# Sparse attention and feed-forward kernel: a pair's value loads requested one step later

## The chip, the cores and the metric

The kernel runs on one core of a Trainium2 chip. A core has a matrix engine (TensorE, PE; its weight loads are listed apart as PEld), a vector engine (VectorE, DVE), a scalar engine (ScalarE, ACT), a general one (GpSimd, POOL) and one that issues transfers (SyncE, SP). Sixteen DMA engines move data between the memories. The metric is the device time of one execution in microseconds; the time given is the median of three runs.

## What is computed

Attention for 4 batches and 8 heads over 768 positions, head size 64, where a query block of 32 positions looks at its neighbours, at the first and last block, and at three sampled blocks; the first and last query block look at everything. The result goes through a feed-forward layer of 512, 2048 and 512 columns. Queries, keys and values are float32; the two weight matrices come as 64-bit floats.

```python
scores = scale * np.matmul(q, k.transpose(0, 1, 3, 2))
scores = np.where(mask, scores, -1000000000.0)
attn = softmax(scores)                 # written out in the reference
x = np.matmul(attn, v)                 # heads put side by side: 3072 x 512
h = x @ w_in
g = h * (1.0 / (1.0 + np.exp(-1.702 * h)))
out = g @ w_out
```

## The kernel before

**Units, items, entries.** Two neighbouring query blocks are a unit of 64 positions. A unit of one batch is an item. Items go in twos: the items of two batches at the same positions use one entry of keys (`kent`) and one of values (`vent`), which below is called a pair. Eight units, 512 rows, are a chunk; there are six chunks. The first chunk is the first four pairs (entries 0 to 3), the fifth pair (entry 4) is items 8 and 9 and begins the second chunk.

**A pair's values** are three transfers: `gather` makes two indirect ones on POOL (L256), 128 rows of 4 KB each, 512 KB, by sampled row numbers into `vown`; `load_own` makes a plain one on SP (L251), 64 rows of 4 KB, 256 KB, into `vmid`. The rows of the first and last block in `vmid` stay between loads. **A pair's keys** (`load_k`) are nine requests on SP: the queries `qt` (L209), two of `kg` (L213, L214), six single sampled blocks (L227), each with a number read from memory first. Entries from the fifth on share two buffers; a pair may be requested when the pair that had its buffer before has been used.

**Order.** The order of all instructions is written out, engine by engine. `first` runs the attention of the first chunk by a table; it also requests the fifth pair's keys. Then `run` goes through steps: `tick(m)` computes one sixteenth of a chunk's feed-forward layer (one block of 128 of the 2048 columns: `up` at L572 to L574, `gate`, and for the step before it `down`, at L617 in the first eight steps), and between these the attention of the next chunk, item by item as `plan` has set it: scores (L304), transposes (L355), products with the values (L379), a turn (L444). Item 8's values are in step 3, item 9's in step 5.

**Loads.** In every quarter of a step `begin` calls `loads`, which requests all pairs that are free, keys and values in turn, up to the entry number in `self.most`. At first it is five for both, so that in step 0 only the fifth pair's values are requested. Before step 1 (`m == 1`) the limit is lifted.

**Weights.** `weights` is a generator that fetches the blocks of both weight matrices by POOL (L477, 512 KB each, into `win` or one of three buffers `raw`) and turns their 64-bit numbers into a high and a low 32-bit part by ACT (L489, L534) and DVE (L493 to L521). `tick` pulls it a few places at a time, between the other work; a place that begins a block also issues the request five blocks ahead. A converted second-matrix block is stored to `ws` by SP (L527).

**Queues.** An engine takes its instructions in order, a request that waits for a buffer included. The profile lists POOL's requests under the DMA queue q0 and SP's under q1.

Of the kernel before, what the change touches and what calls it, by code (L numbers as in the profile page):

```python
# [43 lines left out]
FIRST = CU // 2  # L44
# [5 lines left out]
class Kernel:  # L50
# [4 lines left out]
    def __init__(self, ctx, tc, q, qd, kb, kT, v, vd, sb, w_in, w_out, out):  # L55
        self.tc, self.nc = tc, tc.nc
        self.q, self.qd, self.kb, self.kT, self.v, self.vd, self.sb = q, qd, kb, kT, v, vd, sb
        self.w64, self.out = (w_in.bitcast(I32), w_out.bitcast(I32)), out
        pool = lambda name, bufs, **k: ctx.enter_context(tc.tile_pool(name=name, bufs=bufs, **k))
        self.const = pool("const", 1)  # L60
        self.work = pool("work", 2)
        self.small = pool("small", 6)
        psum = pool("psum", 1, space=PSUM)
        dram = pool("dram", 1, space=DRAM)
        self.ws = [dram.tile([P, DM], F32, name=f"ws{f}") for f in range(NF)]
        self.bank = [psum.tile([P, 512], F32, name=f"bank{i}") for i in range(8)]
        c = self.const


        self.sbr = c.tile([1, NB, NR, 2], I32, name="sbr")  # L70
        self.zero = c.tile([P, 1], F32, name="zero")
        self.seen = c.tile([P, 2 * NPAIR], F32, name="seen")
        self.ident = c.tile([P, P], F32, name="ident")
        self.vidx = c.tile([P, 2, NB], I32, name="vidx")
        self.bias = c.tile([P, NU, 8], F32, name="bias")
        c.tile([P, 56], F32, name="pad")

        self.kg = [c.tile([P, 12, 2, NPAIR * BLK], F32, name=f"kg{i}") for i in range(RING)]
        self.qt = [c.tile([P, 2, NPAIR * UT], F32, name=f"qt{i}") for i in range(RING)]
        self.vown = [c.tile([P, 2, 2 * DM], F32, name=f"vown{i}") for i in range(RING)]  # L80
        self.vmid = [c.tile([P, 2 * DM], F32, name=f"vmid{i}") for i in range(RING)]
        self.win = [None] * NF
        self.x = [tuple(c.tile([P, NCT, CT], F32R, name=f"x{part}0") for part in ("hi", "lo"))]


        more = c.tile([P, 2 * NCT * CT], F32, name="x1")
        nk, nq = 24 * NPAIR * BLK, 2 * NPAIR * UT
        for flat in (more[:, 0:nk], c.tile([P, 2 * WRING * DM], F32, name="wout")):
            self.kg.append(flat.rearrange("p (n b c) -> p n b c", n=12, b=2))
        self.qt += [more[:, nk + nq * i:nk + nq * (i + 1)].rearrange("p (b c) -> p b c", b=2) for i in range(2)]  # L90
        c.tile([P, 16], F32, name="shift")
        spare = [c.tile([P, 2 * DM], F32, name=f"win{NF - 1 - i}") for i in range(6)]
        self.vblocks = [[t[:, j] for j in range(2)] for t in self.vown] + [spare[0:2], spare[2:4]]
        self.vmid += spare[4:6]
        self.kmidof, self.vmidof = [None] * FIRST, [None] * FIRST
        self.units, self.kent, self.vent, self.items = [], [], [], []

        def entry(of, **more):
            of.append({"n": len(of), "scores": 0, "values": 0, **more})
            return of[-1]  # L100

        def item(k, v, **more):
            k["scores"] += 1
            v["values"] += 1
            self.items.append({"n": len(self.items), "unit": self.units[-1], "k": k, "v": v, **more})

        for b0 in range(0, B, 2):
            for u in range(NU):
                k, v = (entry(of, b=b0, u=u) for of in (self.kent, self.vent))
                for b in (b0, b0 + 1):  # L110
                    entry(self.units, b=b, u=u)
                    item(k, v, first=True, end=True)
            for b in (b0, b0 + 1):
                entry(self.units, b=b, u=None)
                k = entry(self.kent, b=b, u=None)
                for i in range(2):
                    v = entry(self.vent, b=b, u=None, i=i)
                    for half in range(2):
                        item(k, v, i=i, half=half, first=i + half == 0, end=i + half == 2)
        for of in (self.kent, self.vent):  # L120
            for e in of:
                e["at"] = e["n"] if e["n"] < FIRST else e["n"] % RING
        self.knext = self.vnext = FIRST
        self.most = {"scores": FIRST + 1, "values": FIRST + 1}
        self.early, self.turned = True, False


# [782 lines left out]
```

## Time and profile before

| what | value |
|---|---|
| median of 3 runs | 759.45 us (758.43 to 759.71) |
| the profiled execution | 758.66 us, span 757.0 us |
| PE busy | 729.5 us, 96% of the span |
| DVE busy | 406.4 us, 54% |
| ACT busy | 374.9 us, 50% |
| POOL busy | 68.5 us, 9% |
| DMA | 126.87 MB, mean 168 GB/s |
| granted PE clock | 0.996 |

The span is the time from the first to the last instruction of the profiled execution. Times below are counted from its start. PE is the engine that is busy longest; a share of busy time is a mean over the first chunk, the steps and the end, so the rows below are of single stretches.

### The profile page before, as it was taken

The page shows a single profiled execution, that of the slowest core. Times are in us where ns is not written, and L with a number is a line of the kernel's source. Part 1 is how long each engine was busy: PE and PEld are TensorE (multiplying, and loading weights), DVE is VectorE, ACT ScalarE, POOL GpSimd, SP SyncE. Part 2 cuts the span into 40 slices and gives each one's busy share as a digit, 9 for nine tenths or more (in the row PEclk, how much of TensorE's full clock was granted, in tenths as well). Part 3 has the DMA queues.
Part 4 walks back from the last instruction along what each step waited for, and adds up shares of the span by engine and source line. Part 5 has one row for each costly group of instructions (what it writes and reads, how often), then busy time and mean ns, then how long its engine had stood idle before and what let it go on. Part 6 is the DMA issues. An engine that isn't in the chain of part 4 may idle for free.

```text
span 757.0 us, 18902 instructions
## 1 busy us (share of the span) xinstructions
PE 729.5 (96%) x7424; PEld 562.2 (74%) x7424; DVE 406.4 (54%) x1069; ACT 374.9 (50%) x938; POOL 68.5 (9%) x111
## 2 busy tenths in 40 slices
PE   3879999999999999999999999999999999999997
PEld 1555666777787777778878878878777777888885
DVE  4578988885554434554454554454555444443333
ACT  3666666764554443545445445445545444433232
POOL 5422212020000000000000000000000000000000
PEclk9999999999999999999999999999999999999999
DMA  8998996676742547565445465345564331141111
GB/s 263 318 389 294 347 310 211 229 227 180 256 162 71 162 140 228 148 174 169 127 126 168 133 173 169 124 125 170 165 216 157 92 101 32 39 112 43 53 45 55
DMA packets 64250, 126.87 MB, mean 168 GB/s; under 512 B 7617, under 2 KB 30402, under 8 KB 63650
## 3 DMA queue, kind: packets, MB, share of 16 engines
q1 hardware_dynamic: 51922, 83.72, 36.5%
q0 software_dynamic: 11376, 41.03, 16.0%
q8 instruction: 58, 0.95, 0.5%
q10 hardware_dynamic: 864, 0.93, 0.4%
q14 instruction: 30, 0.25, 0.1%
HBM read 115.16 MB, written 10.49 MB: 166 GB/s over the span
## 4 chain that ended last, share of the span: by engine, by line
PE 91%; DVE 3%; DMA 2%; ACT 2%; SPq 1%; issue 1%; ACTq 0%; DVEq 0%
PE bank L572 12%; PE bank L573 11%; PE bank L574 11%; PE bank L632 10%; PE bank L628 10%; PE bank L633 10%; PE bank L355 6%; PE bank L379 5%; PE bank L304 5%; PE bank L617 3%; PE bank L444 2%; PE bank L399 2%; PE bank L316 2%; DMA x<-in_kb_dram 1%; DMA scratch<-in_sampled_blocks_dram 1%
## 5 line engine op out<-in xcount | busy, mean ns | idle before, releaser
L587 DVE SCALAR_TENSOR_TENSOR g<-g,bank 128x512 f32<-128x512 f32 x83 | 57.0, 687 | 166.7 <-ACT g L580 166.6
L339 ACT ACTIVATE ex<-bank,nm 128x256 f32<-128x256 f32 (+1 forms) x176 | 84.6, 489 | 117.6 <-DVE nm L327 114.7
L632 PE MATMUL bank<-wout,ghi 128*128 128x512 f32 x352 | 139.2, 395 | 0.0
L633 PE MATMUL bank<-wout,ghi 128*128 128x512 f32 x352 | 136.7, 388 | 0.0
L580 ACT ACTIVATE g<-bank 128x512 f32<-128x512 f32 x96 | 57.4, 598 | 147.2 <-PE bank L574 147.2
L555 DVE TENSOR_TENSOR wout<-wst,wout 128x512 fp32r<-128x512 f32 x80 | 55.3, 692 | 78.7 <-ACT wout L554 76.5
L628 PE MATMUL bank<-wout,glo 128*128 128x512 f32 x352 | 97.0, 388 | 0.0
L327 DVE CUSTOM_DVE_ANT_1 bank<-bank,bias 128x256 f32<-128x256 f32 x176 | 73.7, 440 | 21.9 <-PE bank L304 8.6
L572 PE MATMUL bank<-xhi,win 128*128 128x512 f32 x192 | 79.7, 415 | 0.5 <-ACT xhi L451 0.5
L594 ACT CAST ghi<-g 128x512 fp32r<-128x512 f32 x88 | 54.7, 621 | 49.8 <-DVE g L587 49.7
L572 PE MATMUL bank<-x,win 128*128 128x512 f32 x192 | 77.7, 405 | 0.2 <-DVE g L587 0.2
L628 PEld LDWEIGHTS bank<-wout,glo 128*128 128x128 f32 x352 | 66.1, 188 | 13.8
L632 PEld LDWEIGHTS bank<-wout,ghi 128*128 128x128 f32 x352 | 66.1, 188 | 13.0
L633 PEld LDWEIGHTS bank<-wout,ghi 128*128 128x128 f32 x352 | 66.2, 188 | 12.7
L573 PE MATMUL bank<-xlo,win 128*128 128x512 f32 x192 | 74.9, 390 | 0.0
L574 PE MATMUL bank<-xhi,win 128*128 128x512 f32 x192 | 74.8, 390 | 0.0
L574 PE MATMUL bank<-x,win 128*128 128x512 f32 x192 | 74.7, 389 | 0.0
L573 PE MATMUL bank<-x,win 128*128 128x512 f32 x192 | 74.7, 389 | 0.0
L256 POOL DMA_INDIRECT vown<-in_v_dram,vidx x40 | 38.8, 969 | 375.1 <-PE bank L379 262.8
L360 ACT COPY pt<-bank 128x512 f32<-128x512 f32 (+1 forms) x112 | 56.8, 563 | 20.3 <-PE bank L355 20.1
L602 DVE TENSOR_TENSOR glo<-g,ghi 128x512 fp32r<-128x512 f32 x88 | 60.2, 684 | 1.4 <-ACT ghi L594 1.4
L304 PE MATMUL bank<-kg,qt 64*32 64x256 f32 x1280 | 47.3, 399 | 11.7 <-DMA vmid<-in_v_dram 11.4
(135 smaller groups left out, 1045.1 us busy)
## 6 DMA issues: line engine op xcount, KB each, us to landing
wst<-ws SPq DMA_DIRECT2D x80, 256.0 KB
kg<-in_kb_dram SPq DMA_DIRECT2D x114, 128.0 KB
kg<-in_kb_dram SPq DMA_DIRECT2D x42, 256.0 KB
win<-in_moe_w_in_dram POOLq DMA_DIRECT2D x16, 512.0 KB, 6.7
raw<-in_moe_w_out_dram POOLq DMA_DIRECT2D x16, 512.0 KB, 7.9
kg<-in_kT_dram SPq DMA_DIRECT2D x4, 1536.0 KB
vown<-in_vd_dram SPq DMA_DIRECT2D x8, 768.0 KB
out_dram<-raw SPq DMA_DIRECT2D x41, 128.0 KB
```

The source lines that it names most:

```text
L304: nc.tensor.matmul(sps[h][BLK * c:BLK * (c + 1), n * i:n * (i + 1)].rearrange("p (g n s) -> p g n s", g=2, s=BLK), self.qt[r][rows, bi, UT ...
L327: nc.vector.tensor_tensor_reduce(out=at, in0=at, in1=bias, scale=-SCALE, scalar=3.0e38, op0=ALU.add, op1=ALU.min, accum_out=un["nm"][:, ha ...
L339: nc.scalar.activation(out=ex, in_=sps[h][:, n * k:n * (k + 1)], func=AF.Exp, bias=un["nm"][:, half, c:c + 1], scale=-1.0, accum_out=un["r ...
L572: nc.tensor.matmul(to, wih[:, k], xh, start=(k == 0), stop=False)
L573: nc.tensor.matmul(to, wih[:, k], xl, start=False, stop=False)
L574: nc.tensor.matmul(to, wil[:, k], xh, start=False, stop=(k == NCT - 1))
L580: nc.scalar.activation(out=g, in_=self.h, func=AF.Tanh, scale=0.851)
L587: nc.vector.scalar_tensor_tensor(out=g, in0=g, scalar=1.0, in1=h, op0=ALU.add, op1=ALU.mult)
L602: self.nc.vector.tensor_tensor(out=glo, in0=g, in1=ghi.bitcast(F32), op=ALU.subtract)
L628: nc.tensor.matmul(to[n], glo[:, tk[n]], woh, start=False, stop=last)
L632: nc.tensor.matmul(to[n], ghi[:, tk[n]], woh, start=(f == 0), stop=False)
L633: nc.tensor.matmul(to[n], ghi[:, tk[n]], wol, start=False, stop=False)
```

## The change

One number is lowered by one: the limit of pairs whose values may be requested before step 1.

```diff
--- before.py
+++ after.py
@@ -121,7 +121,7 @@
             for e in of:
                 e["at"] = e["n"] if e["n"] < FIRST else e["n"] % RING
         self.knext = self.vnext = FIRST
-        self.most = {"scores": FIRST + 1, "values": FIRST + 1}
+        self.most = {"scores": FIRST + 1, "values": FIRST}
         self.early, self.turned = True, False
```

`loads` finds nothing to request in step 0. In the first quarter of step 1, with the limit lifted, it requests the sixth pair's keys, the fifth pair's values and the sixth pair's values, in that order. Between the two places the weight generator has been pulled, so requests of its own stand ahead now.

On POOL, about the end of the first chunk (`vown_104` is the fifth pair's gathers, `vown_105` the sixth's, `win` and `raw` are weights; - is before, + after):

```order
 L477 DMA win_1019<-in_moe_w_in_dram 128x1024
 L477 DMA raw<-in_moe_w_out_dram 128x1024
+L477 DMA win_1142<-in_moe_w_in_dram 128x1024
+L477 DMA raw<-in_moe_w_out_dram 128x1024
+L477 DMA win_1177<-in_moe_w_in_dram 128x1024
 L256 DMA vown_104<-in_v_dram,vidx 128x1024 x2
-L477 DMA win_1145<-in_moe_w_in_dram 128x1024
-L477 DMA raw<-in_moe_w_out_dram 128x1024
-L477 DMA win_1180<-in_moe_w_in_dram 128x1024
 L256 DMA vown_105<-in_v_dram,vidx 128x1024 x2
```

The fifth pair's gathers go behind three more weight requests, and stand right ahead of the sixth pair's.

On SP, at the place where the first converted block is stored (`vmid_106` is the fifth pair's plain load):

```order
 L227 ISA
 L227 DMA kg_100<-in_kb_dram 128x256
-L251 DMA vmid_106<-in_v_dram 64x1024
 L527 DMA ws_69<-ghi 128x512
 L209 DMA qt_103<-in_q_dram 128x512
```

The fifth pair's load is gone from ahead of that store and of the sixth pair's keys.

On SP, at the end of the sixth pair's keys (`vmid_107` is the sixth pair's plain load):

```order
 L227 ISA
 L227 DMA kg_101<-in_kb_dram 128x256
+L251 DMA vmid_106<-in_v_dram 64x1024
 L251 DMA vmid_107<-in_v_dram 64x1024
 L527 DMA ws_70<-glo 128x512
```

It stands there now, right ahead of the sixth pair's own.

## Rows read from the trace of the kernel before

**Rows 1.** The page: PE's busy tenths in 40 equal slices.

```profile
PE   3879999999999999999999999999999999999997
```

**Rows 2.** Chain of waits, 62 to 122 us: start, length, what.

```profile
77.00 1.02 PE bank L304 x32
78.02 1.03 PE bank L379 x64
...
89.95 1.38 PE bank L304 x32
...
91.37 1.10 PE bank L379 x64
```

**Rows 3.** POOL's timeline: start, length, line, operation, [idle time before, releaser].

```profile
39.13 0.53 POOL L477 DMA_DIRECT2D raw<-in_moe_w_out_dram  x1 [0.49 <-DMA win<-in_v_dram,vidx]
41.40 0.98 POOL L256 DMA_INDIRECT vown<-in_v_dram,vidx  x1 [1.74 <-PE bank L444]
...
43.82 0.59 POOL L477 DMA_DIRECT2D win<-in_moe_w_in_dram  x1
60.33 0.56 POOL L477 DMA_DIRECT2D raw<-in_moe_w_out_dram  x1 [15.92 <-ACT a L489]
...
61.72 1.14 POOL L256 DMA_INDIRECT vown<-in_v_dram,vidx  x1 [0.30 <-issue]
...
65.90 0.57 POOL L477 DMA_DIRECT2D raw<-in_moe_w_out_dram  x1 [1.77 <-ACT ghi L489]
```

**Rows 4.** The timeline of SP's requests, the same columns.

```profile
54.14 0.50 SPq L251 DMA_DIRECT2D vmid<-in_v_dram  x1
...
62.39 6.15 SPq L227 DMA_DIRECT2D kg<-in_kb_dram  x6
68.64 0.48 SPq L251 DMA_DIRECT2D vmid<-in_v_dram  x1
```

**Rows 5.** ACT's largest wait, 40 to 100 us: us, times, longest.

```profile
ACT win L534 <- DVE a L521: 11.4, 8, 1.9
```

**Rows 6.** DMA queues, 66 to 72 us: packets, MB, share of engines.

```profile
q0 software_dynamic: 516, 1.87, 76.1%
q1 hardware_dynamic: 633, 0.59, 28.4%
```

**Rows 7.** DMA requests issued from 59.7 to 77 us: count, KB each.

```profile
kg<-in_kb_dram SPq DMA_DIRECT2D x6, 128.0 KB
ws<-ghi SPq DMA_DIRECT2D x2, 256.0 KB
kg<-in_kb_dram SPq DMA_DIRECT2D x2, 256.0 KB
qt<-in_q_dram SPq DMA_DIRECT2D x1, 256.0 KB
vmid<-in_v_dram SPq DMA_DIRECT2D x1, 256.0 KB
```

**Rows 8.** DMA queue q1, 59.7 to 73 us.

```profile
q1 hardware_dynamic: 1186, 1.50, 36.9%
```

**Rows 9.** DMA queue q1, 59.7 to 76 us.

```profile
q1 hardware_dynamic: 1654, 2.12, 43.8%
```

**Rows 10.** DMA queues, 94 to 100 us.

```profile
q0 software_dynamic: 362, 1.33, 81.9%
q1 hardware_dynamic: 78, 0.26, 19.3%
```

**Rows 11.** Timeline of PE's weight loads, at item 9's values.

```profile
91.37 0.16 PEld L379 LDWEIGHTS bank<-vmid,pt 128*32 128x32 f32 x8 [0.52 <-DVE x L452]
```

**Rows 12.** The chain of waits at 121 us, then PE's timeline at 142 us.

```profile
121.27 0.58 ACT wst L585
...
142.05 0.32 PE L379 MATMUL bank<-vmid,pt 128*32 128x64 f32 x8 [1.14 <-DVE x L452]
```

**Rows 13.** PE's timeline, before the first down products.

```profile
62.05 3.70 PE L617 MATMUL bank<-ghi,g 128*128 128x512 f32 x8 [0.80 <-DVE g L587]
```

## The prediction

> **What bounds the kernel now.** I read the page's slices first [rows 1]: TensorE (PE) is at nine tenths or more in all but the first three and the last, so what waits there is, lies before some 60 us. Second, the chain of waits, from 62 us on: it runs along PE without a break, through the values of item 8 (first unit of the second chunk, pair entry 4: the fifth pair), which PE starts at 78.02 [rows 2]. So after 62 us whatever holds PE up is paid in full, unless PE would have waited anyway soon after. Third, who requests what and when: GpSimd's (POOL's) timeline [rows 3] and SyncE's (SP's) [rows 4]. Last, the DMA queues by stretch: q0 carries POOL's requests and q1 SP's.
>
> The fifth pair's values are three transfers. Two gathers on POOL (L256, into vown) start at 41.40 and right behind it. One is a plain load of 64 rows on SP (L251, into vmid), issued at 54.14 [rows 3, 4]. Item 8 needs all three at 78.02: its first products read vmid. They have 37 and 24 us, so no wait shows.
>
> **What the change moves, and its price.** No instruction is added or taken away.
>
> *POOL.* Three weight requests (win, raw, win) come ahead of the two gathers. The first of them, at 43.82 now, moves up behind the request of 39.13, some 4 us earlier. The second waits for a free buffer until ACT has read one: it starts at 60.33 after 15.92 us of waiting, and stays there, since ACT's work is not moved; the third follows it. Then come the fifth pair's gathers, from 61.72 on, where the sixth pair's stand now, and the sixth pair's behind them. A gather takes POOL 1.14 us and a pause of 0.30, so four are over at about 67.5: raw, at 65.90 now, goes 1.6 us later [rows 3]. ACT and VectorE (DVE) do not feel these times: between 40 and 100 us their lists of waits name no DMA; ACT's largest there is for DVE [rows 5]. So the earlier weight gains nothing: price 0, covered by conversions that wait for engines.
>
> Are the gathers late? In q0 they stand behind raw and win: 4 requests of 512 KB, 2.10 MB, until they are in. Between 66 and 72 us q0 moves 1.87 MB in 6 us, 0.31 MB a us [rows 6], and the first of the four is requested at 60.33. Even if q0 began with them at 66 only, they would be in at 66 + 2.10 / 0.31 = 72.8: 5 us to spare, price 0.
>
> *SP.* The vmid load for the fifth pair goes behind the nine requests that fetch the sixth pair's keys, of which the last six take SP from 62.39 to 68.54. So it takes the place where the sixth pair's vmid is issued now, 68.64 [rows 4], which is 14.5 us later and 9.4 us before it is needed. The question is when it lands. Ahead of it in q1, from 59.7 us on: a 256-KB store of weights, 256 KB of q, two loads of 256 KB and six of 128 KB of keys, 1792 KB or 1.84 MB; with its own 256 KB, 2.10 MB [rows 7]. In the kernel before q1 has moved 1.50 MB by 73 us [rows 8] and 2.12 MB by 76 us [rows 9]: the load in this slot is through at about 75.9 us, 2.1 us before the need.
>
> But that held because q0 ran dry. While both queues are full, between 66 and 72 us, q1 gets 0.59 MB in 6 us, 0.098 MB a us, for its small packets [rows 6]; from 73 to 76 us it moved 0.62 MB, 0.21 a us [rows 8, 9]. In the changed kernel the two gathers that were requested at 41 to 43 us stand in q0 now: 1.05 MB more, 3.4 us of q0 at 0.31 MB a us, so q0 stays full from 73 on to where its next requests follow. Then the 0.34 MB of keys left at 73 us take 0.34 / 0.098 = 3.4 us, until 76.4. The 0.26 MB of vmid follow, in 4-KB packets like q0's. At an even share of the 0.41 MB a us that both moved [rows 6] they take 1.3 us: 77.7 us, no stall. That is the low end. The high end is the nearest row for this very transfer: the same load, issued at 92.42 with nothing ahead of it in q1, needs the whole stretch from 94 to 100 us for its 0.26 MB, beside 1.33 MB of q0 [rows 10]. Six us from 76.4 gives 82.4, a stall of 4.4 us. I take the middle, 80.0 us, because the first is a mean over 16 engines where PE waits for the last, and the second is a stretch with less throughput than this one. Stall: 80.0 - 78.02 = 2.0 us.
>
> *What of it is given back.* PE has one wait soon after: item 9's values at 91.37 are held by DVE (x L452, 0.52 us at the weight load) [rows 11]. Without it PE would have gone on at 89.95 + 1.02 = 90.97, the time that the same scores take at 77.00 [rows 2], so 0.4 us. DVE comes to that operation late because of the conversions queued ahead of it, which do not hang on item 8's values; I take it that it stays where it is, so 0.4 us of the stall is absorbed. From there the chain is PE without a wait until it passes to ACT (copy at 121.27), then DVE, and comes back to PE at 142.05, where PE waited 1.14 us for DVE [rows 12]. That wait gives nothing back, as DVE's chain itself starts from PE's late result.
>
> Sum: +2.0 - 0.4 = +1.6 us; ends 0 and 4.4 - 0.4 = +4.0 us.
>
> [...] In 66 to 72 us the two queues pass 516 and 633 packets [rows 6], about one for one, so a request on SP's queue slows when POOL's is full. [...]
>
> **The rivals.**
> (a) *The load lands in time* (not slower). The even share holds for all 16 engines, or q0 falls dry for a while: landed by 78.4, a stall under 0.4 us, absorbed at 91.37. For it: the 2.1 us to spare today, and 77.7 us by the arithmetic. Against: 94 to 100 us. It decides at 78.4 us. Time as now, 759.45.
> [...]
> (c) *Faster.* q0 and q1 are relieved of 1 MB between 43 and 58 us; if a conversion or a copy there paced itself by a DMA, PE's first chunk would end sooner. Nothing in the waits says so [rows 5]; PE's own wait where that chunk ends, before the first down products, bounds its price: 0.80 us [rows 13], so 758.65.
>
> **How the numbers follow.** The profiled execution took 758.66 us (span 757.0, 1.66 around it); the median shown is 759.45, 0.79 above it. 758.66 + 1.6 + 0.79 = 761.05. A measurement of this kernel tells some 0.2% from no change, 1.5 us: slower is above 760.97, faster below 757.93. Chances: a stall of 0.4 to 3.5 us as worked out, 0.60; (a) 0.20; (b), or the passage as slow as in 94 to 100 us, 0.15; (c) 0.05. The middle of the first lies just over the edge of slower, so I split it, 0.35 above and 0.25 below; with (b) slower has 0.50. (a) and the lower part of the first are within, 0.45. Faster is (c), 0.05, which would have to exceed its bound or meet with scatter. The range goes from the load in time with the shown scatter of half a us, 759.0, to the full passage, 758.66 + 4.0 + 0.79 = 763.45.
>
> **What would show it.** Right: in the profile after, PE idle before L379 at about 78 us, 1 to 4 us, released by the DMA vmid<-in_v_dram; SP's two vmid loads next to each other at 68.6 and 69.2; POOL's gathers at 61.7 to 66; q0 full through 73 to 76 us; the wait at 91.37 gone; PE's steps from 92 us on later by the stall less 0.4. Wrong: no wait there (a), a wait on vown (then the gathers' landing was mis-sized), a different wait of PE between 62 and 140 us, or first down products before 62.05.

## The result, and the profile after

The changed kernel takes 764.41 us (median of 4, 763.2 to 765.24) where the kernel before takes 759.1 (median of 4, 758.43 to 759.71): a ratio of 1.0068, with a 95% interval of 1.0048 to 1.0089. It is slower, by 5.3 us where 1.6 was forecast, and 0.96 us beyond the upper end of the range (763.45). The profiled execution took 763.2 us with a span of 761.6, against 758.66 and 757.0 before.

The page of after first, its span, PE's line, the granted clock and the DMA share in 40 slices:

```profile
span 761.6 us, 18903 instructions
PE   2879799999999999999999999999999999999997
PEclk9999999999999999999999999999999999999999
DMA  8988976765842437555435455435564230141111
```

Beside [rows 1] one digit has changed where the pair's values are used: the fifth slice (76 to 95 us) has a 7. A slice is 19 us, so this is a few us at one place. The clock's tenths show nothing, because a slice is too coarse for what happened there.

The chain of waits of after, 60 to 98 us (start, length, what), answers to [rows 2]:

```profile
68.18 13.20 DMA vmid<-in_v_dram
81.38 0.04 issue
81.42 1.57 PE bank L379 x64
83.00 4.79 PE bank L617 x8
...
95.06 1.02 PE bank L304 x32
96.08 1.03 PE bank L379 x64
```

The chain no longer runs along PE here. It leaves PE for a DMA: the fifth pair's vmid, requested at 68.18 and in at 81.38 (68.18 + 13.20). PE's timeline of after shows the first down products, which end the first chunk, and the same wait from PE's side, before the first eight products of item 8 (start, length, line, operation, [idle time before, releaser]):

```profile
61.53 3.70 PE L617 MATMUL bank<-ghi,g 128*128 128x512 f32 x8 [0.81 <-DVE g L587]
...
76.46 1.09 PE L304 MATMUL bank<-kg,qt 64*32 64x256 f32 x32
81.42 0.32 PE L379 MATMUL bank<-vmid,pt 128*32 128x64 f32 x8 [3.87 <-DMA vmid<-in_v_dram]
```

So PE waited 3.87 us. But that is not all. Behind the wait the values took 1.57 us where they took 1.03 [rows 2], and the eight down products 4.79. The stretches of after say why (engine columns are busy us and instructions; then the granted clock, the DMA engines' busy share, and GB/s):

```profile
core 0: us, PE busy (x) PEld busy (x) DVE busy (x) ACT busy (x) POOL busy (x), PEclk, DMA share, GB/s
70.00:77.50 7.50, 7.50 (x59) 4.45 (x57) 6.39 (x17) 6.45 (x17) 1.05 (x2) 1.00 1.05 406
77.50:81.40 3.90, 0.05 (x8) 0.00 (x0) 3.45 (x8) 1.32 (x3) 1.05 (x2) 1.00 1.01 266
81.40:85.30 3.90, 3.88 (x67) 2.51 (x68) 3.55 (x11) 3.09 (x10) 0.00 (x0) 0.56 1.04 401
85.30:100.00 14.70, 14.70 (x145) 9.38 (x144) 10.64 (x26) 6.68 (x18) 4.21 (x6) 1.00 0.87 328
```

Two things are to be seen. From 81.4 to 85.3 us, right behind PE's 3.87 us of idling, the granted clock is 0.56 on the mean; it is 1.00 before the wait and 1.00 again from 85.3 to 100 us. And while PE waited, the DMA engines were busy all the time (1.01) but moved 266 GB/s, against 406 just before and 401 just after. The kernel before, in the two middle stretches:

```profile
77.50:81.40 3.90, 3.90 (x94) 2.20 (x77) 3.43 (x9) 1.84 (x4) 1.05 (x2) 1.00 1.03 381
81.40:85.30 3.90, 3.90 (x16) 2.64 (x16) 3.68 (x13) 2.84 (x10) 0.00 (x0) 1.00 1.03 390
```

The two queues' requests stand where they were expected. SP's and POOL's timelines of after, which answer to [rows 3, 4]:

```profile
61.85 6.23 SPq L227 DMA_DIRECT2D kg<-in_kb_dram  x6
68.18 1.14 SPq L251 DMA_DIRECT2D vmid<-in_v_dram  x2
59.80 0.53 POOL L477 DMA_DIRECT2D raw<-in_moe_w_out_dram  x1 [17.74 <-ACT a L489]
61.15 1.19 POOL L256 DMA_INDIRECT vown<-in_v_dram,vidx  x1 [0.30 <-issue]
```

The bill of the profiled run, matmul by matmul against before: 3.87 of wait, and 0.54 (values, 1.57 - 1.03) and 1.16 (down products, 4.79 against 3.63 in the two chains) of slow clock, is 5.57. At item 9 values follow scores at once now (95.06 + 1.02 = 96.08), so the 0.40 that PE lost there before [rows 2, 11] is given back. The first chunk was 0.52 shorter in this run (first down products at 61.53, in [rows 13] at 62.05). 5.57 - 0.40 - 0.52 = 4.65, and the spans differ by 4.6.

That 0.52 is chance, and it matters for how runs are compared. (The prediction has first down products before 62.05 among the signs of being wrong. In a second profile of the same kernel, after_again below, they start at 63.91.) The first chunk's length changes from one run to the next: the first down products of item 6 start between 59.80 and 65.15 us in the profiles of this study, in no order by kernel. So where single profiles are compared below, times are counted from that product's start ("from D"). Before, item 8's values start at 77.95 - 62.05 = 15.90 us from D by PE's timeline (the chain has 78.02), and the span has 757.0 - 62.05 = 694.95 us left from D.

### The profile page after: what moved, and what is told of

Same layout as the page of the kernel before. It is cut to its first block, busy times and chain, and to the rows that moved or that the text cites. A ratio compares the mean times of both kernels' runs of the same rounds, so it can differ in the third digit from the quotient of the medians.

```text
span 761.6 us, 18903 instructions
## 1 busy us (share of the span) xinstructions
PE 729.7 (96%) x7424; PEld 562.2 (74%) x7424; DVE 407.0 (53%) x1069; ACT 375.1 (49%) x938; POOL 69.3 (9%) x111
## 4 chain that ended last, share of the span: by engine, by line
PE 90%; DMA 3%; DVE 2%; SPq 2%; issue 1%; ACT 1%; another core or an unknown queue 1%; ACTq 0%; DVEq 0%
PE bank L572 12%; PE bank L573 11%; PE bank L574 11%; PE bank L632 10%; PE bank L628 10%; PE bank L633 10%; PE bank L355 6%; PE bank L379 6%; PE bank L304 5%; PE bank L617 3%; PE bank L444 2%; PE bank L399 2%; DMA vmid<-in_v_dram 2%; PE bank L316 2%
```

## The experiments

**One half alone: the gathers.** Theory: all of the loss comes from SP's order. The kernel before, with POOL's half of the change only:

```diff
-        self.load_own(e)
-        self.gather(e)
+        for load in ((self.load_own, self.gather) if e["n"] != FIRST else (self.load_own,)):
+            load(e)
...
+            if self.vnext == FIRST + 1 and free(self.vent, self.vnext, "values"):
+                self.gather(self.vent[FIRST])
```

> Only the half of the change that lies on POOL: the fifth pair's gathers go behind the three weight requests, while its 64 rows (vmid) are requested in step 0 as before. My theory: the wait at item 8's values comes from the vmid load alone, which stood behind the sixth pair's keys beside a full q0. Then PE has no wait there, vmid lands at about 60 us, the gathers at about 70, and the time is that of the kernel before, 759.1 within 0.8 us. Rival 'gathers': the three weight requests ahead of the gathers are the cause, and PE waits 3 to 4 us here too: 763 to 765 us.

Measured 758.23 us against 758.66 of before on the same chip (a median of 25, by chance the time of the first profile too), ratio 0.9996 (0.998 to 1.0011). PE's timeline of this kernel has item 8's values right behind its scores:

```profile
78.14 1.09 PE L304 MATMUL bank<-kg,qt 64*32 64x256 f32 x32
79.16 0.32 PE L379 MATMUL bank<-vmid,pt 128*32 128x64 f32 x8
```

Gathers behind three more weight requests, and the weight that is requested earlier, cost and gain nothing by themselves.

**The other half alone: the rows of vmid.** The same edit, with `gather` and `load_own` exchanged.

> Only the half that lies on SP: the 64 rows (vmid) go behind the sixth pair's keys, the gathers stay in step 0. My theory: with the 1 MB of gathers out of q0 at 61 to 74 us, the load lands at about 77.8 us, where the sixth pair's load in that place landed in the kernel before, and PE's wait at item 8 is 0 to 0.8 us: 759.1 to 760 us. Rival 'place': the place behind the keys is enough, PE waits 3 to 4 us and its clock falls: 763 to 765 us.

Measured 760.37 us against 758.66, ratio 1.0028 (1.0004 to 1.0053). PE waits, but half as long as in after, and the granted clock stays at 1.00 (PE's timeline, then stretches of this kernel):

```profile
80.02 0.32 PE L379 MATMUL bank<-vmid,pt 128*32 128x64 f32 x8 [1.85 <-DMA vmid<-in_v_dram]
81.06 3.70 PE L617 MATMUL bank<-ghi,g 128*128 128x512 f32 x8
74.00:80.00 6.00, 4.17 (x46) 2.67 (x44) 5.12 (x11) 4.67 (x9) 1.05 (x2) 1.00 1.05 262
80.00:84.00 4.00, 3.98 (x71) 2.38 (x72) 3.70 (x12) 1.66 (x8) 0.00 (x0) 1.00 1.04 382
```

So it was more than the 0 to 0.8 us that my theory gave to the place alone, and less than the rival's 3 to 4. Both halves are needed for the whole wait: SP's order makes the load late, and POOL's extra requests make it later. The DMA queue q1 tells how, first of this kernel (D at 62.12) from 59.8 to 76 us, then of after (D at 61.53) from 59.2 to 76.4 (packets, MB, share):

```profile
q1 hardware_dynamic: 1675, 2.08, 43.0%
q1 hardware_dynamic: 1489, 1.78, 32.5%
```

1.84 MB stand ahead of the load [rows 7]. Here they are through before 76 us; in after they are not at 76.4, since q0 has 1.05 MB more to move in that time. Even so this load was not in at 76 + a little but at 79.98, where its wait in the chain ends. Its own passage is slow: 262 GB/s.

**SP's order undone alone.** After, with the fifth pair's values requested ahead of the sixth pair's keys in step 1; POOL's order is that of after.

```diff
+            if self.vnext == FIRST and free(self.vent, self.vnext, "values"):
+                self.load_v(self.vent[self.vnext])
+                self.vnext += 1
             if free(self.kent, self.knext, "scores"):
```

> The changed kernel with one order turned: in step 1 the fifth pair's values are requested ahead of the sixth pair's keys, not behind them. vmid is issued at about 59.7 us and lands at 64 to 66. My theory: no wait at item 8, 759.1 within 0.8 us, and the sixth pair's keys land 0.7 us later, which nobody waits for. Rival 'gathers' or 'full queues': the time stays at 763 to 765 us, since q0 is as full as in the changed kernel.

Measured 758.41 us against 758.66, ratio 0.9997 (0.9979 to 1.0014). The values start at 81.07 with D at 65.15, 15.92 from D, as before. The whole loss is gone when SP's order alone is undone.

**Half of the keys ahead.** After, with the load put between the two groups of three sampled keys of the sixth pair:

```diff
         if e["n"] >= FIRST or e["n"] == 0:
+            self.load_own(self.vent[FIRST]) if e["n"] == FIRST + 1 else None
             self.sampled(e, 1, nc.sync if e["n"] else nc.scalar)
...
-        self.load_own(e)
+        self.load_own(e) if e["n"] != FIRST else None
```

> After, with the fifth pair's vmid load requested after the first three of the six sampled keys of the sixth pair, in place of behind all six; gathers and weights as in after. Theory (the packets of keys ahead of it in SP's queue set when it passes): 0.39 MB less stand ahead, which at 0.1 to 0.2 MB a us is 2 to 4 us, so it lands at 77.5 to 79.5, PE waits 0 to 2 us with no half clock behind, and the time is 0 to 2 us above before. Rival (its own passage beside a full q0 is the slow part, and the place does little): the wait is 2.5 us or more and the time 3 us or more above before.

Measured 758.47 us against 757.63 of before on that chip, ratio 1.001 (0.999 to 1.003). SP's and PE's timelines:

```profile
62.55 2.65 SPq L228 DMA_DIRECT2D kg<-in_kb_dram  x3
65.30 0.50 SPq L252 DMA_DIRECT2D vmid<-in_v_dram  x1
66.66 2.69 SPq L228 DMA_DIRECT2D kg<-in_kb_dram  x3
78.24 0.32 PE L379 MATMUL bank<-vmid,pt 128*32 128x64 f32 x8
```

No wait: three keys (0.39 MB) fewer ahead are enough, as the theory has it; values start 15.93 from D (62.31). The load passes slowly here too (292 GB/s in 74 to 77 us), but early enough.

**The clock.** After, with four added matmuls of 128x512 ahead of item 8's values, so that PE idles less while it waits. It was run twice, the second time with after itself beside it.

```diff
         if self.sparse(g):
+            [nc.tensor.matmul(un["av"], self.ident, g["pt"][0].rearrange("p k s -> p (k s)")) for _ in range(4 if g["n"] == CU else 0)]
             def product(i, h, k, c, n):
```

> The changed kernel with four added products of 128x512 (float32, written to item 8's bank before its values, results overwritten) ahead of item 8's values, some 3.6 us of PE's time by the rate of L617, in place of PE's wait of 3.9 us. My theory: PE's granted clock does not fall to one half after 81 us, since PE was not idle; item 8's products take 1.0 us and the first down products 3.6, not 1.6 and 4.8; the rest of the wait is about 0.3 us, so the time is 1.7 us below the changed kernel, 762.7 us. Rival: the slow stretch after the wait has another cause (the DMA's writes), it stays, and the time is that of the changed kernel, 764.4, or above it by the part of the added work that isn't hidden.

> The changed kernel once more, beside the next three on the same chip. PE waits 3 to 4.5 us for vmid before item 8's values, the granted clock is half for some 3.4 us behind that wait, and the time is 4 to 6 us above the kernel before (ratio 1.005 to 1.008). If the loss of the first comparison came from the chip and not from the wait, the time is within 2 us of before although the wait stands in the trace.

> After, with four added matmuls of 128x512 ahead of item 8's values (they write a bank of sums before its first product clears it, so nothing else is changed), now on the same chip as after. Theory (the half clock behind the wait is a loss of its own): the remaining wait is about 1 us, the clock stays full behind it, and the time is 1 to 2 us below after_again. Rival (the slow clock's loss is given back later, at a wait for another engine): the clock stays full all the same, but the time is within 0.5 us of after_again.

The first time (without after on its chip) it measured 764.52 us, ratio 1.0087 (1.0066 to 1.0108) to before: no less than the 764.41 of after elsewhere, where a gain was looked for. That total settles nothing, although the clock stayed full behind the wait (1.00 from 85 to 88.4 us in its profile). Side by side, after took 764.76 us (1.0095, 1.0072 to 1.0118), 7.1 above before and so more than the 4 to 6 expected, and the filled kernel 761.9 (1.006, 1.0042 to 1.0078). The four added products are listed as eight matmuls at L374. PE's timeline of after_again and a stretch of it, then the same of the filled kernel:

```profile
63.91 3.70 PE L617 MATMUL bank<-ghi,g 128*128 128x512 f32 x8 [0.80 <-DVE g L587]
84.32 0.32 PE L379 MATMUL bank<-vmid,pt 128*32 128x64 f32 x8 [4.38 <-DMA vmid<-in_v_dram]
85.91 4.76 PE L617 MATMUL bank<-ghi,g 128*128 128x512 f32 x8
84.30:87.70 3.40, 3.38 (x66) 2.26 (x67) 2.49 (x8) 3.05 (x10) 0.00 (x0) 0.55 1.03 403
```

```profile
63.05 3.70 PE L617 MATMUL bank<-ghi,g 128*128 128x512 f32 x8 [0.69 <-DVE g L587]
78.99 3.70 PE L374 MATMUL bank<-pt,ident 128*128 128x512 f32 x8
84.13 0.32 PE L379 MATMUL bank<-vmid,pt 128*32 128x64 f32 x8 [1.45 <-DMA vmid<-in_v_dram]
85.16 3.70 PE L617 MATMUL bank<-ghi,g 128*128 128x512 f32 x8
84.10:88.30 4.20, 4.17 (x73) 2.40 (x73) 3.12 (x8) 2.59 (x8) 0.71 (x2) 1.00 1.04 405
```

The load was in later in the filled kernel than in after_again (values at 21.08 us from D, against 20.41), and yet its span has less left from D: 761.6 - 63.05 = 698.55 us, against 763.6 - 63.91 = 699.69. Counted from the values' start it is 698.55 - 21.08 = 677.47 against 699.69 - 20.41 = 679.28, 1.8 us less. Behind the wait the values took 85.91 - 84.32 = 1.59 us in after_again and 85.16 - 84.13 = 1.03 in the filled kernel, the down products 4.76 and 3.70: 1.6 us of slow clock, and all of it still stands at the end of the span. So the slow clock is a loss of its own, and is not given back later. The medians differ by 2.9 us, and their intervals overlap a little; the rival (given back) had 0.5 at most. The table below has the same for the other profiles.

**Why the load passes slowly.** It fills 64 rows, partitions 0 to 63 of its tile. In this kernel the rows of the fifth and sixth pair go to every second partition (the values then stand in the wrong rows, so it serves for its time alone):

```diff
-        self.nc.sync.dma_start(out=self.vmid[e["at"]][0:UT], in_=self.v[e["b"] // 2][BLK * q0:BLK * (q0 + 2)])
+        self.nc.sync.dma_start(out=self.vmid[e["at"]][slice(0, P, 2) if e["n"] in (FIRST, FIRST + 1) else slice(0, UT)], in_=self.v[e["b"] // 2][BLK * q0:BLK * (q0 + 2)])
```

> After, with the 64 rows of the fifth and the sixth pair's vmid loads written to every second partition in place of partitions 0 to 63; the values then stand in wrong rows, and no work is added or left out. Theory A (the load passes slowly because all its packets land in one half of the partitions, where they crowd each other): vmid is in by about 79, PE's wait is 0.5 to 1.5 us, no half clock follows, and the time is 2 to 4 us below after_again. Theory B (it passes slowly because both queues are full, wherever it lands): the wait stays 3 to 4.5 us, and the time is within 1 us of after_again.

> The kernel of rows_spread once more, since its wait (3.37 us) fell between both theories while its transfers kept 400 GB/s, and its first chunk ended 2 us earlier than in the runs that it is compared with. Counted from the first down product of item 6, item 8's values start at 19.9 to 21.1 us in the runs of after. Theory A: at 18.5 to 19.6 us here, 0.5 us or more before the earliest of those, again with some 400 GB/s. Theory B: at 19.9 to 21.1 here too, and 3.37 was an early draw.

> Only SP's half of the change (as in e2_rows_late, the gathers stay in step 0), with the 64 rows of the fifth and the sixth pair's vmid written to every second partition; values stand in wrong rows, and no work is added or left out. Theory A (landing in one half of the partitions slows the passage of both queues): the cores' transfers keep near 400 GB/s through 74 to 80 us, where e2_rows_late fell to 320, vmid lands 1 to 2 us sooner, and PE's wait is 0 to 0.9 us in place of 1.85. Theory B (the keys ahead are all that counts): the wait is 1.5 to 2.5 us again.

The first run took 760.92 us (1.0058, 1.0037 to 1.008), 3.8 below after beside it, but its wait was 3.37 us and the half clock came behind it (0.68 on the mean from 81.5 to 85.5 us): the total as theory A has it, the wait between the two theories, and the clock as theory B. The second run took 763.56 (1.0072, 1.0049 to 1.0096), so the gain in the total did not repeat and is not claimed. What did repeat is the rate. PE's timeline and stretches of the second run:

```profile
63.27 3.70 PE L617 MATMUL bank<-ghi,g 128*128 128x512 f32 x8 [0.69 <-DVE g L587]
82.50 0.44 PE L379 MATMUL bank<-vmid,pt 128*32 128x64 f32 x8 [3.20 <-DMA vmid<-in_v_dram]
79.20:82.40 3.20, 0.10 (x8) 0.00 (x0) 2.74 (x6) 1.37 (x3) 1.05 (x2) 0.94 1.04 405
82.40:85.50 3.10, 3.00 (x66) 2.31 (x67) 3.03 (x11) 1.74 (x8) 0.00 (x0) 0.51 1.04 405
```

While PE waits for the load the engines move 405 GB/s, where after moved 266 in its wait. The values start 19.47 and 19.23 us from D in the two runs, against 19.89 to 21.08 in the four of after's order: 0.4 to 1.9 us sooner. All the keys are still ahead of it, and most of the wait is still there. With the keys out of the way sooner (only SP's half of the change), the spread load is worth about 1 us too:

```profile
81.99 0.32 PE L379 MATMUL bank<-vmid,pt 128*32 128x64 f32 x8 [0.94 <-DMA vmid<-in_v_dram]
74.00:80.00 6.00, 6.00 (x33) 3.78 (x35) 4.92 (x12) 5.51 (x15) 0.65 (x2) 1.00 1.04 390
```

0.94 us of wait in place of 1.85, 390 GB/s in place of 262 (393 from 77 to 83 us, which lies as far behind this profile's D, 65.09, as 74 to 80 us does with the rows late), and 758.32 us against 758.26 (1.0001, 0.9988 to 1.0015). The 320 of the expectation is the rate with the rows late from 77.5 to 81.5 us. Theory A holds for the rate, and for about 1 us of the wait in single profiles; its first expectation, a wait of 0.5 to 1.5 us with all the keys ahead, was too much.

All profiles together ("from D" as above; the second column says how many of the sixth pair's keys stand ahead of the load, and whether the fifth pair's gathers come late and so fill q0; the last is the difference of two others):

| kernel | keys ahead; q0 | values from D | PE's wait | clock behind it | span left from D | left from the values |
|---|---|---|---|---|---|---|
| before | none | 15.90 | 0 | 1.00 | 694.95 | 679.05 |
| gathers late | none, more in q0 | 15.94 | 0 | 1.00 | 694.08 | 678.14 |
| rows first | none, more in q0 | 15.92 | 0 | 1.00 | 694.25 | 678.33 |
| rows midway | half, more in q0 | 15.93 | 0 | 1.00 | 694.59 | 678.66 |
| rows late, spread | all | 16.90 | 0.94 | 1.00 | 694.51 | 677.61 |
| rows late | all | 17.90 | 1.85 | 1.00 | 695.58 | 677.68 |
| after, spread (two runs) | all, more in q0 | 19.47, 19.23 | 3.37, 3.20 | half | 698.80, 698.43 | 679.33, 679.20 |
| after (two runs) | all, more in q0 | 19.89, 20.41 | 3.87, 4.38 | half | 700.07, 699.69 | 680.18, 679.28 |
| after, filled (two runs) | all, more in q0 | 20.57, 21.08 | 0.95, 1.45 | 1.00 | 698.03, 698.55 | 677.46, 677.47 |

The last column sets the clock's part apart from the wait's. The four profiles with a wait and a full clock behind it have 677.46 to 677.68 us left, the four with the half clock 679.20 to 680.18: at least 1.5 us more, to the end of the span. One thing disturbs the column. The two profiles of the first comparison, before and the first of after, have a pause that none of the other ten has: the values of one item, at 153.77 and 158.49 us on PE's timeline, take 2.29 and 1.92 us until the next down products start, with 0.70 and 0.39 us of idling that is put down to "issue", where gathers late takes 1.03. Without these 1.26 and 0.89 us before would have 677.79 left and after 679.29. What made the pause is not known; as both profiles have it, it hardly changes their difference.

## Why the prediction was right and wrong

**What bounds the kernel: right.** PE is the path from 62 us on, and what held it there was paid in full, less what item 9's wait gave back.

**POOL's part at price 0: right.** The three weight requests and four gathers started at the times that were worked out (raw at 59.80, the gathers from 61.15; D was 0.52 earlier than in the trace of before), no wait names vown, and the half alone measured no change. Beside SP's half it does cost: its 1.05 MB in q0 make the wait 3.87 and 4.38 us where the rows alone have 1.85. The prediction has that in SP's part.

**SP's part, the mechanism: right.** The load stands behind the keys, the keys behind a full q0 (1.35 MB from 73 to 77.2 us, where before it moved 0.26 from 73 to 76), and PE behind the load. The three terms of its price, though, each fell on the same side. The wait is what they add up to. The DMA queues of after, first q1 from 59.2 to 73 us, then both from 73 to 77.2, then both from 77.2 to 81.4:

```profile
q1 hardware_dynamic: 1184, 1.49, 34.4%
...
q0 software_dynamic: 367, 1.35, 78.9%
q1 hardware_dynamic: 370, 0.38, 25.5%
...
q0 software_dynamic: 168, 0.59, 53.4%
q1 hardware_dynamic: 213, 0.56, 49.3%
```

The 0.34 MB of keys that were to be left at 73 us were left (1.49 MB moved, 1.50 assumed), and went at 0.38 / 4.2 = 0.090 MB a us where 0.098 was taken: they were out near 77, not 76.4 (a mean over the engines: the DMA view of 77.2 to 81.4 us still counts 18 packets of between 512 B and 2 KB, as the keys' are). That is 0.6 us. PE needed the load at 81.42 - 3.87 = 77.55, not 78.02, as its first chunk was shorter: 0.5 us.

**The term that was mis-sized: the passage of the load itself.** It was given 3.6 us (76.4 to 80.0), the middle of 1.3 and 6. It took 4.4 (77 to 81.38). The middle had no reason of its own, and the row for the high end, 94 to 100 us [rows 10], was the better measure. I set it aside as "a stretch with less throughput" (264 GB/s there), but the low throughput was the load's own doing: when its rows go to partitions 0 to 63 beside a full q0, all transfers together move 266 GB/s in after and 262 with the rows late, and with the rows on every second partition 405 and 390. Why the place matters is not shown. q0's requests, which fill all 128 partitions, are slowed too: 0.14 MB a us (0.59 in 4.2) from 77.2 to 81.4 us, where they had 0.32 (1.35 in 4.2) from 73 to 77.2.

The rate alone does not make 4.4 us. In 77.2 to 81.4 us q1 moved 0.56 MB, more than twice the load's 0.26: so by these bytes, an estimate, the sixth pair's 64 rows, requested right behind, pass in the same time, while PE waits for its own load until 81.38. Why it was in so late stays open; the load of 94 to 100 us, with nothing behind it there, was no faster.

With these, 0.6 + 0.8 + 0.5 above the 2.0 forecast is the 3.9 us of the trace. The split between the keys and the load rests on the 77, a mean.

**The term that was missing: TensorE's clock.** The sum ended with the wait. PE came out of it at half clock (0.56 on the mean from 81.4 to 85.3 us) and lost 1.7 us more (0.54 + 1.16). The trace of before had a warning in it. PE starts there only at 11.39 us, pauses again before 17.7, and the clock is half from 17.7 to 21.1 (PE's timeline, then stretches):

```profile
11.39 3.22 PE L304 MATMUL bank<-kg,qt 64*32 64x256 f32 x49 [11.39 <-DMA vmid<-in_v_dram]
14.20:17.70 3.50, 2.02 (x27) 0.85 (x22) 2.56 (x11) 1.55 (x7) 2.55 (x6) 1.00 0.99 293
17.70:21.10 3.40, 3.40 (x52) 1.98 (x60) 1.58 (x9) 3.16 (x12) 2.72 (x4) 0.50 1.04 386
```

PE is idle for 1.48 of the 3.5 us ahead of 17.7, and at 0.50 behind it while it is busy throughout. Taken at half the work, 3.40 us of busy time at 0.50 are a loss of 1.7 us, an estimate. That row does not say whether a wait of 2 to 4 us brings it about, but it is reason enough to put the loss into the range. A range whose upper end is a long wait had to have this term behind it: 4.0 + 1.7 would have made that end 758.66 + 5.7 + 0.79 = 765.15, and held the time. With the wait as it came, 758.66 + 3.87 + 1.70 - 0.40 + 0.79 = 764.6, against a median of 764.41.

**What is given back at item 9, 0.4: right** (0.40). PE's wait of 1.14 us at 142 us [rows 12] gave nothing back, as forecast: it is 1.15 us in after.

**The rivals.** (a), in time, fell: it took an even share of 0.41 MB a us. The share was about even (0.59 and 0.56 MB from 77.2 to 81.4), but both queues together moved 0.27 MB a us there. For (b) there is no measurement: no run shows how the engines divide their time between two queues, only what passed (367 and 370 packets from 73 to 77.2 us, 168 and 213 from 77.2 to 81.4, q0 first). The other half of its chance of 0.15, a passage as slow as in 94 to 100 us (a stall of 4.4), came nearest to the 3.87. (c) fell: the half of the change that it speaks of measured nothing.

## What to carry to other kernels

A load that moves to a later place in a queue is priced by what stands ahead of it in its own queue and by the other queues that are full at that time (here item 8's values start 15.93 us from D with half of the keys ahead, 19.89 and 20.41 with all of them, and 17.90 with all of them and 1.05 MB less in q0), and its own passage by the nearest row of the same load under the same conditions, not by an even share of a rate that other loads had. The granted clock behind the wait is to be read too: here it was 0.56 behind 3.87 us of waiting, and the slow work was a second term, 1.7 us on 3.9. Four products in the wait saved it (1.00 behind). The cheapest cure is the order itself: three transfers fewer ahead of the load were enough to lose nothing (758.47 us against 757.63, ratio 1.001).

## What was not expected of the hardware

- A load to 64 neighbouring partitions beside a full queue lowered the rate of all transfers from 406 to 266 GB/s while it passed; to every second partition the same bytes passed at 405 and 390.
- At item 8's values, waits of 3.20, 3.37, 3.87 and 4.38 us were followed by the half clock (0.51 from 82.4 to 85.5 us, 0.68 from 81.5 to 85.5, 0.56 from 81.4 to 85.3 and 0.55 from 84.3 to 87.7); waits of 0.94, 0.95, 1.45 and 1.85 us were not (1.00). Early in the first profile of the filled kernel a wait of 2.49 us, in a stretch in which PE idled more than that, stands at the start of 6.8 us at 0.50 (29.2 to 36.0 us).
- The first chunk's length differed by up to 5.35 us between profiles (D at 59.80 and 65.15), in no order by kernel. Slow clock early on is a part of it: from 10 to 36 us the granted clock is 1.00 on the mean in the shortest and 0.87 where D is 65.09. What decides it is open. As the span is D and what is left behind it, totals of a few runs scatter by one or two us here.
